# ScalarE copies of the up half, Sigmoid for tanh, and new engine orders in a transformer block with linear attention and a gated MLP

## Chip, core and metric

The kernel runs on one core of a Trainium2 chip. The metric is the device time of one execution in microseconds (us). Of several executions the median counts. The five engines each work through their own queue in order: TensorE (PE in the profile, with its weight loads as PEld), VectorE (DVE), ScalarE (ACT), GpSimd (POOL) and SyncE (SP), which here issues nearly all DMAs.

## What is computed

The input x is 2048 rows of 448 (bfloat16). A linear attention with 16 heads of 28 and then a gated MLP are added to it, each behind a layernorm:

```python
q, k, v = split_heads(layernorm(x) @ wqkv)
pq, pk  = q @ w_phi, k @ w_phi                      # per head, 28 x 28
phi_q   = concat(softmax(pq), softmax(-pq))         # phi_k in the same way
kv, z   = sum_s phi_k[s]^T v[s], sum_s phi_k[s]
h       = x + concat_heads((phi_q @ kv) / (phi_q @ z + 1e-6)) @ wo
n       = layernorm(h)
out     = h + (sigmoid(n @ w_gate) * (n @ w_up)) @ w_down   # 448 -> 1792 -> 448
```

## The kernel before

The 2048 rows are 16 tiles (t = 0 to 15) of 128. The kernel is written as a list of named operations, each with what it reads and writes; from that list the waits on semaphores are derived (a DMA has a semaphore of its own in a ring; whoever needs several loads waits for each). The order of the operations on each engine isn't derived: it is written out by hand in ORDER, one string per engine. An engine does its operations strictly in that order, so one that waits holds up all behind it.

The names that matter below, with the engine and the line of the profile:

- x0 to x14, ld_k, ld_v, ld_q0 to ld_q3 on SP load the input and A_wqkv. The four ld_q are transposing DMAs (L503) into WqT.
- bst, agg, pow1, nm1, nb1, xn (L548 to L579) are the first layernorm on VectorE, GpSimd and ScalarE; xn5 and its like write xn_pad, which has five buffers. xT0 to xT3 transpose it on TensorE (with a copy xT0e to xT3e on ScalarE or VectorE), xT4 to xT15 do so by DMA (L586).
- w2m0_0 to w2m0_3 and w2m1_0 to w2m1_3 (TensorE, L615) fold w_phi into wk and wq. Each w2m1 reads all four parts of WqT. w2e are the copies out of PSUM.
- ppa, ppb, pva, pvb, vva, vvb (TensorE, helper line L329) are the products with Wk and wv: 8 matmuls of 448 columns in the a part, 6 in the b part. The array is used as two halves of 64 rows that write two PSUM banks at the same time; the b part swaps the banks of the halves, so it waits until the a part is done with them. v1_t copies v out of PSUM (L534), ek_t takes exp (L674, L675), ss, rs, phi (L678 to L688) normalise it, kva_t and kvb_t add phi^T v into banks 6 and 7, which seed starts.
- warm0 to warm9 are matmuls on zeros that fill TensorE's time at the start.
- pqa, pqb (TensorE) and eq (ScalarE, L726, exp of 1024 columns) make phi_q; num_t (TensorE) the numerators and sums in banks 6 and 7 (num1 in 2 and 3); rsm, qq, b, c, rden (VectorE, L803 to L811) and o_t (GpSimd or VectorE, L815) the quotient; oT_t its transpose (by DMA from t = 2 on, L828); wof0, wof1, woa, wob (TensorE) the product with wo in banks 2 and 3.
- h_t (VectorE, L841) adds x and gives the row sum; h0 and h1 are copies on ScalarE. nm, sq (ScalarE Square, L847), ve (L850), pow2 (GpSimd, L852), hn (L856) are the second layernorm, hT_t the transpose (by DMA, L864).
- wwo and wgu are operations on TensorE without an instruction: they only wait, for the four loads of wo and for the eight loads of the gate and up weights.
- ga and gb (TensorE, L329) are gate and up of one group: ga0_5 is tiles 0 and 1 (256 columns), column block ff = 5 of 14; the groups of tiles 0 and 2 have 256 columns, those of tiles 4, 8 and 12 have 512. An even ff has its gate in bank 4 and its up half in bank 5, an odd one in banks 0 and 1, so a group can start when the one before the last has been read out. sig (ScalarE, L914) and hh (VectorE, L915) read them out: sig writes sg_sb, which has four buffers, and hh reads sg_sb and the up bank and writes hhT.
- dn, dp, dm, dl (TensorE) are the down product, fin (VectorE, L949) adds it to h, out_t stores.

The operations are made in the order of PROGRAM; ORDER interleaves them, for instance the gate groups of tiles 0 and 1 with num and wo of later tiles. Before, the sigmoid is made as (tanh(g/2) + 1) / 2: hh is (tanh + 1) times up, and fin multiplies by 0.5:

```python
op("act", "sig" + nm, lambda e: e.activation(sg_sb[:, k, 0:N], bk(bg)[:, 0:N], ACT.Tanh, scale=0.5), r=[B(bg)], w=[("sg", k)])
op("dve", "hh" + nm, lambda e: e.scalar_tensor_tensor(out=hhT[(t0 // 4) % NHH][:, ff, ns], in0=sg_sb[:, k, 0:N], scalar=1.0,
                                                      in1=bk(bu)[:, 0:N], op0=ALU.add, op1=ALU.mult), ...)
```

tanh and exp need no change of ScalarE's function tables between them: the trace has one table load, at the start.

Of the kernel before, what the change touches and what calls it, by code (L numbers as in the profile page):

```python
# [1020 lines left out]
```

## Time and profile before

| | us |
|---|---|
| median of 3 runs (lowest, highest) | 203.37 (203.37, 203.64) |
| the profiled execution's own time | 203.38 |
| span from its first to its last instruction | 201.6 |
| TensorE busy in the span | 195.6 |

The granted clock of TensorE is 1.00 throughout. "Busy" counts instructions that are under way; matmuls overlap and their ends are modelled, so busy time says where TensorE stood still, not how fast it was. A row of the table by stages gives the stretch, its length, and then the busy time and count for PE, PEld, DVE, ACT and POOL, the clock, the DMA share and GB/s. A row of a timeline gives start, duration, engine, line, operation, out<-in, and in brackets the idle time ahead of it and what ended it. A row of the waits gives who waited for whom, the total, the times and the longest. A row of the groups gives line, engine, operation, operands and shape, the count, then busy us, mean ns of one, and the idle time before. Names of operations aren't in the trace: they are read off by counting a queue's instructions along ORDER.

### The profile page before, as it was taken

To read this page: it belongs to the slowest core of one execution; us is meant where nothing else is said; L and a number is where in the kernel's file an instruction comes from. 1 tells how busy PE (TensorE), PEld (TensorE's weight loads), DVE (VectorE), ACT (ScalarE), POOL (GpSimd) and SP (SyncE) were. 2 spreads that over 40 slices of the span, in tenths; PEclk is the share of its full clock that TensorE was granted. 3 is DMA by queue.
4 is the path that set the end of the run, shared out by engine and by line. 5 is a ranking of instruction groups with operands and counts; after the bars stand their busy time and mean duration, and the time that the engine had idled before them with its cause. 6 is when DMAs were issued, how large, how long until landed. Compare 5 with 4: busy or idle time off the path is not lost.

```text
span 201.6 us, 5849 instructions
## 1 busy us (share of the span) xinstructions
PE 195.6 (97%) x2500; PEld 114.0 (57%) x2500; DVE 133.1 (66%) x326; ACT 91.7 (45%) x189; POOL 57.4 (28%) x90
## 2 busy tenths in 40 slices
PE   7989999999979999999999999999999999999995
PEld 2935565665558788776444444555555555444443
DVE  6998999978999984496758877436432422272224
ACT  3778988998672663222333442324322212222220
POOL 5689869913531962000041110001400000000000
DMA  6967554919994246130005411030222000004002
GB/s 169 301 136 134 58 80 86 295 55 270 313 204 92 52 57 80 27 41 17 0 3 114 87 31 25 7 71 23 60 49 52 0 0 3 0 3 137 0 0 91
DMA packets 32866, 16.25 MB, mean 81 GB/s; under 512 B 25096, under 2 KB 31944, under 8 KB 32840
## 3 DMA queue, kind: packets, MB, share of 16 engines
q1 hardware_dynamic: 32336, 15.86, 34.9%
q8 instruction: 19, 0.31, 0.7%
q10 hardware_dynamic: 504, 0.03, 0.2%
q14 instruction: 7, 0.06, 0.1%
HBM read 8.34 MB, written 1.84 MB: 50 GB/s over the span
## 4 chain that ended last, share of the span: by engine, by line
PE 89%; SPq 5%; DMA 2%; ACT 2%; issue 1%; DVE 0%
PE psum L329 82%; PE psum L942 5%; SPq L430 3%; DMA WqT<-in_A_wqkv_dram 2%; SPq L503 2%; ACT eq L726 2%; PE psum L890 1%; PE psum L541 0%; DVE v L534 0%; PE psum L615 0%; PE psum L888 0%; DVE x_sb L949 0%
## 5 line engine op out<-in xcount | busy, mean ns | idle before, releaser
L329 PE MATMUL psum<-xnT,wg_sb 64*128 64x512 bf16 (+1 forms) x490 | 93.1, 333 | 0.4 <-ACT eq L726 0.2
L329 PE MATMUL psum<-xnT,wu_sb 64*128 64x512 bf16 (+1 forms) x490 | 92.8, 333 | 0.0
L914 ACT ACTIVATE sg_sb<-psum 128x512 bf16<-128x512 f32 (+1 forms) x70 | 34.9, 511 | 90.5 <-PE psum L329 90.0
L915 DVE SCALAR_TENSOR_TENSOR hhT<-sg_sb,psum 128x512 bf16<-128x512 bf16 (+1 forms) x70 | 39.0, 577 | 53.8 <-ACT sg_sb L914 53.1
L329 PEld LDWEIGHTS psum<-xnT,wg_sb 64*128 64x128 bf16 x490 | 44.5, 94 | 21.5 <-DVE hhT L915 3.1
L329 PEld LDWEIGHTS psum<-xnT,wu_sb 64*128 64x128 bf16 x490 | 44.5, 94 | 12.8
L329 PE MATMUL psum<-wd_sb,hhT 64*128 64x448 bf16 x336 | 36.9, 349 | 0.0
L329 PEld LDWEIGHTS psum<-wd_sb,hhT 64*128 64x128 bf16 x336 | 17.8, 94 | 14.3 <-DVE x_sb L841 0.5
L329 PE MATMUL psum<-wv_sb,xnT 64*128 64x448 bf16 x112 | 22.3, 351 | 0.1
L329 PE MATMUL psum<-Wk,xnT 64*128 64x448 bf16 x112 | 22.1, 350 | 0.2 <-DVE v L534 0.2
L850 POOL TENSOR_SCALAR ve<-ssq 128x1 f32<-128x1 f32 x10 | 2.0, 201 | 61.2 <-ACT junk L847 60.9
L688 POOL TENSOR_TENSOR phi<-hhT,rs 128x896 bf16<-128x896 bf16 x10 | 17.1, 1724 | 2.2 <-PE psum L329 1.4
L678 DVE TENSOR_REDUCE ss<-hhT 128x32 f32<-128x896 bf16 x16 | 16.9, 1067 | 0.3 <-ACT hhT L675 0.3
L726 ACT ACTIVATE eq<-psum 120x1024 bf16<-120x1024 f32 x16 | 15.7, 1032 | 1.0 <-PE psum L329 0.9
L329 PE MATMUL psum<-xnT,Wq 64*120 64x512 bf16 x112 | 14.8, 384 | 0.2
L815 POOL TENSOR_TENSOR o_pad<-c_sb,rden 128x448 bf16<-128x448 bf16 x12 | 11.1, 934 | 13.5 <-DVE rden L811 13.4
L329 PE MATMUL psum<-wo_e,oT 64*128 64x448 bf16 x49 | 11.5, 349 | 0.0
L329 PE MATMUL psum<-wo_o,oT 64*128 64x448 bf16 x49 | 11.5, 349 | 0.0
L942 PE MATMUL psum<-wd_sb,hhT 128*128 128x448 bf16 (+2 forms) x70 | 11.1, 316 | 0.0
L949 DVE SCALAR_TENSOR_TENSOR x_sb<-psum,x_sb 128x448 bf16<-128x448 f32 (+2 forms) x17 | 9.4, 591 | 2.5 <-PE psum L942 1.6
L806 DVE TENSOR_TENSOR b_sb<-psum,qq 128x464 bf16<-128x464 f32 x16 | 10.1, 637 | 0.7 <-PE psum L329 0.4
L329 PEld LDWEIGHTS psum<-Wk,xnT 64*128 64x128 bf16 x112 | 7.6, 94 | 4.9 <-issue 1.4
(107 smaller groups left out, 230.8 us busy)
## 6 DMA issues: line engine op xcount, KB each, us to landing
out_dram<-x_sb SPq DMA_DIRECT2D x15, 112.0 KB, 1.8
...
```

The costliest lines, as they stand in the source:

```text
L329: p = e.matmul(o, lhsT=w, rhs=r, start=st, stop=sp, tile_position=(row, 0))
L430: return op(eng, name, lambda e: e.dma_start(dst, src), r=r, w=w, dma="in" if eng == "sp" else "ain", nring=48 if eng == "sp" else 8, kb=kb)
L503: op("sp", "ld_q%d" % gg, lambda e, gg=gg: e.dma_start_transpose(out=WT[1][:, gg:gg + 1, :], in_=A_wqkv[:, gg * GP:gg * GP + P]), w=[("WqT ...
L678: op("dve", "ss%d" % t, lambda e: e.tensor_reduce(ss[:, s, :].rearrange("p (b h) -> p b h", h=2), eks.rearrange("p b (d h) -> p b h d", h= ...
L688: return e.tensor_tensor(phi[:, sp, :, :, :].rearrange("p b a n -> p (b a) n")[:, :, 0:56].rearrange("p b (d h) -> p b d h", h=2), eks.rea ...
L726: op("act", "eq%d_%d%s" % (c, i, "pm"[sg]), lambda e, sg=sg: e.activation(eq[c][:, sg, 2 * i:2 * i + 2, :].rearrange("p g n -> p (g n)"), ...
L806: op("dve", "b%d" % t, lambda e: e.tensor_tensor(h3(b_sb), OMv[:, :, :, 0:EV], h2(qq)[:, :, :, None].to_broadcast([P, NB, 8, EV]), ALU.mul ...
L815: return e.tensor_tensor(o_pad[:, t % NO, off:off + D].rearrange("p (h d) -> p h d", h=H), c_sb[:, t % NS, :, 0:DH], rden[:, t % NS, :][:, ...
L914: op("act", "sig" + nm, lambda e: e.activation(sg_sb[:, k, 0:N], bk(bg)[:, 0:N], ACT.Tanh, scale=0.5), r=[B(bg)], w=[("sg", k)])
L915: op("dve", "hh" + nm, lambda e: e.scalar_tensor_tensor(out=hhT[(t0 // 4) % NHH][:, ff, ns], in0=sg_sb[:, k, 0:N], scalar=1.0, in1=bk(bu)[ ...
L942: p = e.matmul(bk(b)[:, lo:hi], lhsT=hb[:, ff, TS(t)], rhs=wd_sb[:, ff, lo:hi], start=ff == 0, stop=ff == FT - 1)
L949: op("dve", "fin%d%s" % (t, nm), lambda e: e.scalar_tensor_tensor(out=h_sb[:, t, lo:hi], in0=bk(b)[:, lo:hi], scalar=0.5, in1=h_sb[:, t, l ...
```

## The change

Sigmoid takes the place of tanh, so hh becomes one product and fin multiplies by 1.0. For 26 of the 28 groups of 256 columns (UCOPY: all but 0_0 and 0_1), ScalarE copies the up half out of PSUM to SBUF (uc, into xn_pad, which is free by then), and hh reads two SBUF operands, on VectorE or, for 12 of them, on GpSimd, which ORDER decides. sload is one sigmoid of one column that stands behind the last eq. The four loads of wo share one semaphore, and so do the eight of gate and up. The orders of all engines are new up to about the groups of tile 4; behind that they are the same.

```diff
+        if many is not None:
+            o.sem, o.val = (dma,) + many[:1], 16 * many[1]
...
+        op("act", "sload", lambda e: e.activation(sg_sb[:, 0, 0:1], neghalf[:, 0:1], ACT.Sigmoid), r=["neghalf"], w=[("sg", 0)])
...
-            op("act", "sig" + nm, lambda e: e.activation(sg_sb[:, k, 0:N], bk(bg)[:, 0:N], ACT.Tanh, scale=0.5), r=[B(bg)], w=[("sg", k)])
-            op("dve", "hh" + nm, lambda e: e.scalar_tensor_tensor(out=hhT[(t0 // 4) % NHH][:, ff, ns], in0=sg_sb[:, k, 0:N], scalar=1.0,
-                                                                  in1=bk(bu)[:, 0:N], op0=ALU.add, op1=ALU.mult),
-               r=[B(bu), ("sg", k)], w=[("hh", (t0 // 4) % NHH, ff, t % 4) for t in range(t0, t0 + n)])
+            op("act", "sig" + nm, lambda e: e.activation(sg_sb[:, k, 0:N], bk(bg)[:, 0:N], ACT.Sigmoid), r=[B(bg)], w=[("sg", k)])
+            up, ub = bk(bu)[:, 0:N], B(bu)
+            if nm in UCOPY:
+                j = UCOPY.index(nm) % NX
+                up, ub = xn_pad[:, j, 0:N], ("xn", j)
+                op("act", "uc" + nm, lambda e: e.copy(up, bk(bu)[:, 0:N]), r=[B(bu)], w=[ub])
+            op(("pool", "dve") if nm in UCOPY else "dve", "hh" + nm, lambda e: e.tensor_tensor(
+                hhT[(t0 // 4) % NHH][:, ff, ns], sg_sb[:, k, 0:N], up, ALU.mult),
+               r=[ub, ("sg", k)], w=[("hh", (t0 // 4) % NHH, ff, t % 4) for t in range(t0, t0 + n)])
```

The orders, cut to what is spoken of below:

```diff
 pe (before)
-w2m0_3 warm6 warm7 warm8 ppa0 xT3 ppb0 xT2 warm9 vva0 seed vvb0 ppa2 w2m1_0 w2m1_1 vva2 ppb2 vvb2 kva0 w2m1_3 w2m1_2 pva4 pvb4 kvb1 pva5
-pqb1_1 num0 num1 ... oT1 wwo wof0 wof1 ... hT0 hT1 num6 wgu ga0_1 ga0_0
-ga2_4 ga2_5 gb2_4 gb2_5 dp0_8 dp0_11 ga2_6 ga2_7
 pe (after)
+w2m0_3 warm6 warm7 warm8 warm9 ppa0 xT2 ppb0 vva0 xT3 vvb0 w2m1_1 w2m1_0 ppa2 vva2 ppb2 vvb2 w2m1_2 seed w2m1_3 pva4 kvb0 pvb4 kva1 pva5
+pqb1_1 wwo num0 num1 ... oT1 wof0 wof1 ... hT0 hT1 wgu num6 ga0_1 ga0_0
+ga2_4 dp0_4 ga2_5 gb2_4 dp0_8 gb2_5 dp0_11 ga2_6 ga2_7
 act (before)
-w2e0_0 w2e0_2 w2e0_3 xT3e nm1_4 ek0 ek1 ... ek2 nm1_8 ek3 v1_3
-eq3_0p eq3_0m eq3_1p eq3_1m sig0_1 sig0_0 sig0_3 sig0_2
-sq4 sq5 sig0_11 sig0_10 sq7 sig0_13 sq6 sig0_12 sig2_1
 act (after)
+w2e0_0 w2e0_2 nm1_2 w2e0_3 nm1_3 xT2e ek0 ek1 ... ek2 ek3 v1_3 nm1_8
+eq3_0m eq3_0p eq3_1p eq3_1m sload sig0_1 sig0_0 sig0_3 uc0_3 uc0_2 sig0_2
+sq4 sq5 sig0_13 uc0_12 sig0_12 uc0_13 sq6 sq7 uc2_0 ... uc2_4 sig2_5 uc2_5 uc2_6 sig2_6
 pool (before)
-o0 o1 o2 o3 pow2_0 pow2_1 o4 o5 nm2 o6 o7 pow2_3 ve2 pow2_2 hn3 hn2 ve5 o8 nm4 pow2_4 o9 nm5 pow2_5 pow2_7 pow2_6 ve8
 pool (after)
+o0 o1 o2 o3 pow2_1 pow2_0 o5 o4 o7 ve2 hh0_2 pow2_2 hh0_4 hh0_5 o8 hh0_7 hn2 ve3 pow2_3 hn3 nm6
+o9 ve6 ve4 hh0_12 pow2_6 ve5 hn6 hh2_0 pow2_4 hn4 ve7 pow2_7 pow2_5 hn5 hh2_3 hh2_1 hh2_6 hh2_7 hh2_8 hh2_9 ve8
 dve (after, the hh of UCOPY among them)
+rden7 hh0_3 h2 h3 rden6 o6 rsm8 ... h5 qq9 hh0_6 ... h7 hh0_9 h6 hh0_8 rsm10 rden9 hh0_13 hh0_10 qq10 nm5 hh0_11 nm7 hh2_2
```

SP's order changes only from oT4 on (oT5 oT4 oT7 oT6 oT8 hT2 hT3 ... in place of oT4 oT5 oT6 oT7 hT3 hT2 ...).

More of the change, by code (lines that the diff above doesn't have):

```diff
@@ L28, in __init__, with op @@
         self.where = {n: e for e in ENGINES for n in ORDER[e].split()}
-    def op(self, eng, name, fn, r=(), w=(), dma=None, nring=0, after=(), rows=128, half=None, kb=0, grp=None):
+    def op(self, eng, name, fn, r=(), w=(), dma=None, nring=0, after=(), rows=128, half=None, kb=0, grp=None, many=None):
         o = _Op()
@@ L309 @@
 PACE = {"ld_wg1": "kva14"}
+UCOPY = "0_2 0_3 0_4 0_5 0_6 0_7 0_8 0_9 0_10 0_11 0_12 0_13 2_0 2_1 2_2 2_3 2_4 2_5 2_6 2_7 2_8 2_9 2_10 2_11 2_12 2_13".split()
 PROGRAM = (
@@ L427, in B, with load @@
             return ("bank", i)
-        def load(name, dst, src, w, kb, r=(), eng="sp"):
+        def load(name, dst, src, w, kb, r=(), eng="sp", many=None):
             return op(eng, name, lambda e: e.dma_start(dst, src), r=r, w=w, dma="in" if eng == "sp" else "ain",
-                      nring=48 if eng == "sp" else 8, kb=kb)
+                      nring=(48 if eng == "sp" else 8) if many is None else 0, kb=kb, many=many)
         op("dve", "zero", lambda e: e.memset(zero[:], 0.0), w=["zero"])
@@ L504, in build @@
                 out=WT[1][:, gg:gg + 1, :], in_=A_wqkv[:, gg * GP:gg * GP + P]), w=[("WqT", gg)], dma="tr", nring=64)
-        load("ld_woe0", wo_e[:, 0:3, :], A_wo[0:3 * P, :].rearrange("(kt p) n -> p kt n", p=P), [("wo", 0)], 336)
-        load("ld_woe1", wo_e[0:64, 3, :], A_wo[3 * P:D, :], [("wo", 1)], 56)
-        load("ld_woo0", wo_o[:, 1:4, :], A_wo[64:D, :].rearrange("(kt p) n -> p kt n", p=P), [("wo", 2)], 336)
-        load("ld_woo1", wo_o[64:P, 0, :], A_wo[0:64, :], [("wo", 3)], 56)
+        load("ld_woe0", wo_e[:, 0:3, :], A_wo[0:3 * P, :].rearrange("(kt p) n -> p kt n", p=P), [("wo", 0)], 336, many=(100, 4))
+        load("ld_woe1", wo_e[0:64, 3, :], A_wo[3 * P:D, :], [("wo", 1)], 56, many=(100, 4))
+        load("ld_woo0", wo_o[:, 1:4, :], A_wo[64:D, :].rearrange("(kt p) n -> p kt n", p=P), [("wo", 2)], 336, many=(100, 4))
+        load("ld_woo1", wo_o[64:P, 0, :], A_wo[0:64, :], [("wo", 3)], 56, many=(100, 4))
         wo_keys = [("wo", i) for i in range(4)]
@@ L518, in build @@
                 load("ld_%s%d" % (nm, kt), dst[part, kt, :], src[r0 + part.start:r0 + part.stop, :], [(nm, kt)],
-                     448 * (part.stop - part.start) // P)
+                     448 * (part.stop - part.start) // P, many=(101, 2 * KT))
                 wgu_keys.append((nm, kt))
@@ L949, in finish @@
             op("dve", "fin%d%s" % (t, nm), lambda e: e.scalar_tensor_tensor(
-                out=h_sb[:, t, lo:hi], in0=bk(b)[:, lo:hi], scalar=0.5, in1=h_sb[:, t, lo:hi], op0=ALU.mult, op1=ALU.add),
+                out=h_sb[:, t, lo:hi], in0=bk(b)[:, lo:hi], scalar=1.0, in1=h_sb[:, t, lo:hi], op0=ALU.mult, op1=ALU.add),
                r=[B(b), ("x", t)], w=[("xo", t, lo)])
```

79 rows, old and new, of the table ORDER are left out of this document.

## The prediction

> **What bounds the kernel now.** I read the engine totals first, then the table by stages, then the waits, then the chain of work that ended last.
>
> ```profile
> PE 195.6 (97%) x2500; PEld 114.0 (57%) x2500; DVE 133.1 (66%) x326; ACT 91.7 (45%) x189; POOL 57.4 (28%) x90
> ```
> ```profile
> 20.00:44.00 24.00, 23.94 (x449) 14.75 (x443) 22.50 (x44) 22.10 (x45) 18.59 (x13) 1.00 0.54 119
> ...
> 59.20:76.70 17.50, 17.43 (x320) 14.03 (x322) 15.66 (x52) 8.80 (x26) 10.81 (x19) 1.00 0.38 72
> 76.70:95.00 18.30, 18.30 (x292) 14.31 (x290) 11.67 (x35) 4.92 (x14) 0.31 (x1) 1.00 0.31 42
> ```
> ```profile
> PE psum L615 <- DMA WqT<-in_A_wqkv_dram: 0.7, 1, 0.7
> ```
> ```profile
> 10.72 4.12 DMA WqT<-in_A_wqkv_dram
> ...
> 19.30 24.18 PE psum L329 x431
> ```
>
> The reader is to see three things. TensorE has 0.06 us of idle time between 20 and 44, 0.07 between 59.2 and 76.7 and none between 76.7 and 95: in the two gate stages that the 26 groups belong to (59 to 95), where VectorE is busy 15.66 of 17.5 and 11.67 of 18.3 us, nothing of that reaches TensorE. So relief for VectorE has almost nothing to win there. What TensorE loses, it loses before 20 us, where the chain runs through the last load of WqT, and at a few joints. So the question of this change is what its **new orders** do at those joints.
>
> **The start.** Here are TensorE's instructions around the wait for WqT, and VectorE's one that ends the next wait.
>
> ```profile
> 13.33 0.93 PE L329 MATMUL psum<-Wk,xnT 64*128 64x448 bf16 x8
> 14.98 0.55 PE L615 MATMUL psum<-Wphi,WqT 112*128 112x112 bf16 x8 [0.72 <-DMA WqT<-in_A_wqkv_dram]
> 15.46 0.93 PE L329 MATMUL psum<-wv_sb,xnT 64*128 64x448 bf16 x8
> 16.23 0.73 PE L329 MATMUL psum<-Wk,xnT 64*128 64x448 bf16 x6
> 16.80 0.73 PE L329 MATMUL psum<-wv_sb,xnT 64*128 64x448 bf16 x6
> 17.36 0.28 PE L329 MATMUL psum<-v,phi 64*128 64x58 bf16 x8
> 17.57 0.57 PE L615 MATMUL psum<-Wphi,WqT 112*128 112x112 bf16 x8
> 18.30 0.35 PE L329 MATMUL psum<-Wk,xnT 64*128 64x448 bf16 x1 [0.16 <-DVE v L534]
> ```
> ```profile
> 17.57 0.63 DVE L534 CAST v<-psum 128x448 bf16<-128x448 f32 x1 [0.85 <-PE psum L329]
> ```
>
> By the order of before these are ppa2, w2m1_0 with w2m1_1, vva2, ppb2, vvb2, kva0, w2m1_3 with w2m1_2, pva4. Slots, start to start: vva2 0.77, ppb2 0.57, vvb2 0.56, the pair w2m1_0/1 0.48; ppa2 has as many matmuls of the same width as vva2, so 0.77. The WqT loads keep their place in SP's queue, and w2m1 needs all four, so it can't begin before about 14.98 in either kernel. Before, ppa2 is done under that wait. After, **w2m1_1 and w2m1_0 stand ahead of ppa2**, and seed moves behind the wait too. TensorE then arrives at 13.33 at the latest, where ppa2 starts now, and some 0.2 earlier with seed's two matmuls gone from there: it idles 1.65 to 1.9 us. From 14.98, 0.48 for w2m1 and 0.77 + 0.77 + 0.57 + 0.56 for ppa2, vva2, ppb2, vvb2 bring vvb2's slot to its end at 18.13. v1_2 on VectorE, which frees the bank that pva4 writes, follows 0.2 behind that slot's end (17.57 against 17.36) and pva4 0.73 behind v1_2's start (18.30 against 17.57): pva4 at 19.07, 0.77 later than now. seed and the other w2m1 fit into that step, as kva0 and they do now. A little comes back: pva4 and pvb4 had stood side by side, with a stop for the other half's bank (pvb4 at 19.30, 1.00 after 18.30, against 0.77: 0.23); after, kvb0 stands between them. kva0's 0.21 is still to do and takes the most of it again. I take **+0.7**. Bounds: +0.3 if ppa2's delay is half absorbed behind v1_2, +1.1 if seed and ppa2 come on top whole. Nothing later gives it back, since 20 to 44 has 0.06 us idle. The exchange of two xT and nm1 instructions between ScalarE, GpSimd and VectorE in this stage fills time in which TensorE idles: 0. nm1_8 goes behind v1_3 on ScalarE, and xn8, xn9, phi2 and xn11 on GpSimd and four transposes in SP's queue go later with it; I cost that at 0 too, because TensorE's own shift by 0.7 covers about half and these tiles are made ahead of use; uncovered, pva8 would wait, by an estimate up to 0.5, which the upper bound takes in.
>
> **The gate's first groups.** The wait for eight loads (wgu) becomes one semaphore and moves ahead of num6, under a wait for VectorE's c_sb; wwo likewise moves to where TensorE has a backlog. In exchange ScalarE switches tables once (sload) between the last eq and sig0_1.
>
> ```profile
> 55.41 3.77 ACT L726 ACTIVATE eq<-psum 120x1024 bf16<-120x1024 f32 x4 [0.24 <-PE psum L329]
> 60.64 0.71 ACT L914 ACTIVATE sg_sb<-psum 128x256 bf16<-128x256 f32 x2 [1.46 <-PE psum L329]
> ```
> ```profile
> 61.05 0.75 DVE L915 SCALAR_TENSOR_TENSOR hhT<-sg_sb,psum 128x256 bf16<-128x256 bf16 x2 [0.23 <-ACT sg_sb L914]
> ```
> ```profile
> L476 ACT ACT_TABLE_LOAD x1 | 1.3, 1283 | 3.4 <-DVE mask L468 3.4
> ```
> ```profile
> PEld psum L329 <- DVE c_sb L809: 1.0, 1, 1.0
> ...
> PE psum L329 <- ACT eq L726: 0.2, 1, 0.2
> ```
>
> The last fence is the wait view of 57 to 59.5: num6 waits 1.0 for c_sb, and then TensorE idles 0.2 more between num6 and ga0_1, which I put down to wgu's waits: up to 0.25 to win. ScalarE ends eq at 59.18, has 1.46 us free and starts sig0_1 at 60.64. After: 1.28 for the load and about 0.25 for sload's own one column give 60.7 to 60.8, so sig0_1 starts 0.1 later than now instead of 0.25 earlier, hh0_1 behind it too, and with it the bank that the next odd group needs. The gain of 0.25 and the table cancel: I take **0**, between -0.25 (table wholly covered) and +0.2. The Trainium skill, ScalarE: Activation LUTs, section What ACT_TABLE_LOAD costs, says that a switch is 1283 ns and a drain of about 1380 ns, 2.66 us; the trace agrees on the first (1283) and has no row for the second. By 2.66 this term would be about +1.3 rather than 0.
>
> The joint at 70.5 goes. There the first instruction of woa6 waits for oT7:
>
> ```profile
> 67.96 1.26 SPq L828 DMA_TRANSPOSE oT<-o_pad  x1
> ```
> ```profile
> 70.23 0.27 PE L329 MATMUL psum<-xnT,wg_sb 64*128 64x256 bf16 x1
> 70.54 0.35 PE L329 MATMUL psum<-wo_e,oT 64*128 64x448 bf16 x1
> ```
> ```profile
> oT<-o_pad SPq DMA_TRANSPOSE x14, 2.5
> ```
>
> Issued at 67.96, 2.5 us to land: 70.46, and woa6 at 70.54, when the last gate matmul (70.23 and 0.27) had drained, where undisturbed ones overlap: about 0.2 of the 0.31 between the two starts is lost. After, GpSimd makes o7 right after o4 and VectorE makes o6, so both transposes are issued some 1.5 us sooner: **-0.2**.
>
> **Copies and products.** 26 copies like the sigmoids of 128x256 (0.33 to 0.36 each, since 0.71 covers two) add 8.6 us to ScalarE, whose 59.2 to 95 has 13.7 of 35.8 busy: covered, and banks come free in time (four ScalarE instructions per pair of groups, 1.4 us, against 2.5 of TensorE for each of the seven pairs of the first stage). 26 hh of 417 ns leave VectorE; 14 come back. Their cost isn't in the trace: at least 0.18 (by the row of phi below, 637 x 256/896), at most 0.42; 0.25 taken, as phi too reads SBUF alone. It is on no path. 12 go to GpSimd:
>
> ```profile
> L688 POOL TENSOR_TENSOR phi<-hhT,rs 128x896 bf16<-128x896 bf16 x10 | 17.1, 1724 | 2.2 <-PE psum L329 1.4 <-DVE rs L684 0.7
> ...
> L815 POOL TENSOR_TENSOR o_pad<-c_sb,rden 128x448 bf16<-128x448 bf16 x12 | 11.1, 934 | 13.5 <-DVE rden L811 13.4
> L915 DVE SCALAR_TENSOR_TENSOR hhT<-sg_sb,psum 128x256 bf16<-128x256 bf16 x28 | 10.8, 417 | 7.0 <-ACT sg_sb L914 6.6
> ...
> L847 ACT ACTIVATE junk<-x_sb,sum 128x448 bf16<-128x448 bf16 x14 | 9.2, 659 | 1.1 <-DVE x_sb L841 1.0
> ...
> L852 POOL TENSOR_TENSOR rst<-ve,neghalf 128x1 f32<-128x1 f32 x14 | 7.6, 551 | 0.5
> ...
> L688 DVE TENSOR_TENSOR phi<-hhT,rs 128x896 bf16<-128x896 bf16 x6 | 3.7, 637 | 0.1
> ...
> L850 POOL TENSOR_SCALAR ve<-ssq 128x1 f32<-128x1 f32 x10 | 2.0, 201 | 61.2 <-ACT junk L847 60.9
> ...
> L856 POOL TENSOR_SCALAR hn_pad<-x_sb,nm,rst 128x512 bf16<-128x512 bf16 x2 | 1.5, 770 | 0.0
> ```
>
> 896 columns 1724 ns, 448 columns 934: 1.76 ns a column and 0.14 fixed, so 0.60 us for 256. **GpSimd becomes a queue that reaches TensorE**: sg_sb has four buffers, so sig2_5 must wait for hh2_1, and ga2_7 for sig2_5 and uc2_5. hh2_1 stands behind ve6, ve4, hh0_12, pow2_6, ve5, hn6, hh2_0, pow2_4, hn4, ve7, pow2_7, pow2_5, hn5, hh2_3, and ve6 behind sq6.
>
> ```profile
> 75.06 0.27 PE L329 MATMUL psum<-xnT,wg_sb 64*128 64x256 bf16 x1
> ...
> 85.47 0.27 PE L329 MATMUL psum<-xnT,wg_sb 64*128 64x256 bf16 x1
> ```
> ```profile
> 83.79 0.71 ACT L914 ACTIVATE sg_sb<-psum 128x256 bf16<-128x256 f32 x2 [2.06 <-PE psum L329]
> ```
>
> The first row ends gb0_12 at 75.33, the second starts ga2_7. After gb0_12 ScalarE has uc0_12, sig0_12, uc0_13 (1.1) and sq6 (0.66): 77.1. GpSimd's list: 4 ve (0.8), 4 pow2 (2.2), 3 hn (2.3), 4 hh (2.4) make 7.7: hh2_1 ends near 84.8 to 84.9. sig2_5, which would start near 84.7 (0.57 later than the 84.1 that the row of 83.79 gives, as dp0_8, six matmuls like ppb2's, is put ahead of gb2_5), goes to 84.95 with uc2_5, uc2_6 and sig2_6 queued behind it, uc2_5 ends near 85.7, ga2_7 at 85.77: **+0.3**, between 0 and +0.9 (next part). tanh and Sigmoid, and hh on PSUM as one product, I cost alike (0); factor 0.5 in fin too.
>
> **Sum** against the profiled execution's own 203.38 (span 201.6 and 1.8 around it; the median of the runs is 203.37): 0.7 + 0 - 0.2 + 0.3 = +0.8. **Forecast 204.2 us**, likeliest range 203.8 to 204.8.
>
> **Rivals.** *The wait for WqT isn't longer* (the other side). WqT's last load was issued at 10.72 and took 4.12. If such a transpose landed in the 2.8 us that the ones of xnT take,
>
> ```profile
> xnT<-xn_pad SPq DMA_TRANSPOSE x12, 2.8
> ```
>
> it would be there at 13.5, 1.3 earlier, and the order that starts w2m1 first would gain: 0.7 - 1.3 + 0.1 gives **202.9**. It decides from a landing before 14.0 on, 0.8 earlier than now. For it: the wide spread of such loads; against: SP's queue in front of it is unchanged. *Half paid*: the start costs 0.3 and the table hides, so the joints outweigh: 0.3 - 0.25 - 0.2 + 0.1, **203.3**. *GpSimd's queue is slower than its rows*: in before, a GpSimd phi that ran beside a VectorE phi shows a pair of 3.71 where two means make 3.45, and a pair of xn 1.88 against 1.54 for two of hn's 770, which has the same size.
>
> ```profile
> 34.06 3.71 POOL L688 TENSOR_TENSOR phi<-hhT,rs 128x896 bf16<-128x896 bf16 x2
> 18.54 1.88 POOL L579 TENSOR_SCALAR xn_pad<-x_sb,nm,rst 128x512 bf16<-128x512 bf16 x2
> ```
>
> At 0.3 for each of two or three VectorE products that fall into that queue, ga2_7 is 0.6 to 0.8 later yet: **204.9**. The Trainium skill, SBUF — State Buffer, section Who interferes with whom, says it as a rule: a VectorE instruction with two SBUF inputs and a GpSimd instruction that reads SBUF exclude each other. The two rows agree. *The switch is longer*: if ScalarE stands still around the load for as long again as it lasts (1.28), sig0_1, hh0_1 and ga0_3 are 1.3 later: 204.2 + 1.3, **205.5**; for it, no row shows a load with work in flight; against, the one load there cost 1283 ns. *It doesn't do what it says*: were Square not in Sigmoid's table, 14 squares at two loads of 1.28 add 36 us to ScalarE, and the time is over 210.
>
> **Chances.** Forecast 0.49, GpSimd's queue 0.10, longer switch 0.06, tables flipping 0.02, WqT early 0.18, half paid 0.15. About 0.2%, 0.41 us, is what a measurement of this kernel can tell from no change. Slower (above 203.78): nearly all of the forecast with the three behind it, 0.66; within 0.2%: 0.16; faster: 0.18. The range from 202.9 to 205.3 leaves out the two long-table cases and half of the early one.
>
> **What would show it.** The wait of L615 for WqT in the after trace: 1.7 to 2.0 us (0.72 now), and pva4 near 19.1; if that wait is under 1.0, the forecast falls. ACT_TABLE_LOAD twice, the second at 59.9 to 61.5 (all marks after 20 us lie 0.8 later than now). No idle time ahead of woa6. A wait of sig2_5 for GpSimd's hh, and TensorE idle 0.2 to 0.5 us ahead of ga2_7. The stage after 95 us keeps its length.

## The result and the profile after

The changed kernel takes **204.74 us** (median of 22 runs, 204.12 to 205.90), the kernel before 203.69 us on the same chip (22 runs, 203.05 to 205.91): a ratio of 1.005, 95% interval 1.0032 to 1.0069. It is 1.05 us slower; 0.8 was forecast. The kernel before stands 0.3 higher in this series than in the 3 runs that the forecast of 204.2 started from, so it is the differences that are compared. A second series on another occasion (the run e5_changed_again below) gives 204.42 against 203.39, +1.03.

The profiled execution of the first series took 205.90 us, the slowest of its 22 runs. The totals of its page:

```profile
PE 195.4 (96%) x2500; PEld 112.7 (55%) x2500; DVE 127.1 (62%) x310; ACT 99.8 (49%) x217; POOL 67.1 (33%) x106
```

VectorE has 6.0 us less to do, ScalarE 8.1 and GpSimd 9.7 more, and TensorE as much as before. To see what TensorE makes of that, cut both traces at the same instructions of TensorE: pva4, num0, then hT1, dn0_0, ga4_1 and the end. These are the tables by stages of before, then of the changed kernel (its second profile, of 204.08 us). The columns are those of the prediction's table; the second number is the length of the stretch.

```profile
18.30:45.73 27.43, 27.30 (x505) 16.64 (x507) 25.82 (x50) 25.30 (x53) 20.23 (x15) 1.00 0.55 117
57.32:75.15 17.83, 16.66 (x325) 13.57 (x324) 16.49 (x53) 9.41 (x26) 9.37 (x15) 1.00 0.47 98
75.15:94.85 19.70, 19.70 (x308) 15.17 (x306) 12.57 (x39) 6.18 (x19) 1.86 (x5) 1.00 0.30 42
94.85:201.60 106.75, 104.29 (x1024) 52.57 (x1020) 52.28 (x111) 30.26 (x58) 7.74 (x18) 1.00 0.15 36
```

```profile
18.74:46.17 27.43, 27.37 (x514) 16.94 (x514) 26.13 (x50) 25.34 (x54) 21.09 (x16) 1.00 0.58 117
57.70:75.01 17.31, 16.35 (x327) 13.75 (x325) 14.56 (x48) 12.51 (x36) 9.63 (x15) 1.00 0.45 105
75.01:95.56 20.55, 19.81 (x309) 13.96 (x306) 7.99 (x29) 11.17 (x38) 11.41 (x21) 1.00 0.17 35
95.56:202.30 106.74, 104.28 (x1024) 52.58 (x1022) 52.61 (x112) 30.27 (x58) 7.75 (x18) 1.00 0.15 36
```

The reader is to see that the attention stage and everything behind ga4_1 keep their length to 0.01 us. The first gate stage is 0.52 us shorter, the second 0.85 us **longer**, although VectorE is busy 4.6 us less in it: TensorE was never idle there before and now is for 0.7. Between num0 and hT1, which the tables leave out, 57.70 less 46.17 is 11.53, where before had 57.32 less 45.73, 11.59: -0.06. From pva4 to the end that makes -0.06 - 0.52 + 0.85 - 0.01, **+0.26**. The remaining 0.8 of the 1.05 lie ahead of pva4.

There the first profile shows the wait that the prediction is about, and the instructions behind it (w2m1_1 and w2m1_0, ppa2, vva2, ..., vvb2, and pva4):

```profile
15.19 0.55 PE L619 MATMUL psum<-Wphi,WqT 112*128 112x112 bf16 x8 [1.43 <-DMA WqT<-in_A_wqkv_dram]
15.68 0.93 PE L333 MATMUL psum<-Wk,xnT 64*128 64x448 bf16 x8
...
17.77 0.73 PE L333 MATMUL psum<-wv_sb,xnT 64*128 64x448 bf16 x6
18.43 0.37 PE L619 MATMUL psum<-Wphi,WqT 112*128 112x112 bf16 x4
...
19.34 0.36 PE L333 MATMUL psum<-Wk,xnT 64*128 64x448 bf16 x1
```

The wait is 1.43 us (0.72 before), ppa2 begins at 15.68 instead of 13.33, and pva4 at 19.34 instead of 18.30. The second profile, whose last WqT arrived earlier, has the same picture with less wait:

```profile
14.59 0.55 PE L619 MATMUL psum<-Wphi,WqT 112*128 112x112 bf16 x8 [0.66 <-DMA WqT<-in_A_wqkv_dram]
```

In the second gate stage, these are GpSimd's queue from ve6 and ve4 to hh2_3 and hh2_1, ScalarE's sig2_5 and uc2_5, and TensorE's last matmul of ga2_6 and first of ga2_7, all in the first profile:

```profile
78.66 0.46 POOL L854 TENSOR_SCALAR ve<-ssq 128x1 f32<-128x1 f32 x2 [0.61 <-ACT junk L851]
79.18 0.67 POOL L925 TENSOR_TENSOR hhT<-sg_sb,xn_pad 128x256 bf16<-128x256 bf16 x1
79.80 0.57 POOL L856 TENSOR_TENSOR rst<-ve,neghalf 128x1 f32<-128x1 f32 x1
80.45 0.19 POOL L854 TENSOR_SCALAR ve<-ssq 128x1 f32<-128x1 f32 x1
80.73 0.77 POOL L860 TENSOR_SCALAR hn_pad<-x_sb,nm,rst 128x512 bf16<-128x512 bf16 x1
...
85.10 0.77 POOL L860 TENSOR_SCALAR hn_pad<-x_sb,nm,rst 128x512 bf16<-128x512 bf16 x1 [0.18 <-POOL rst L856]
85.83 1.29 POOL L925 TENSOR_TENSOR hhT<-sg_sb,xn_pad 128x256 bf16<-128x256 bf16 x2
```
```profile
87.22 0.38 ACT L919 ACTIVATE sg_sb<-psum 128x256 bf16<-128x256 f32 x1 [1.16 <-PE psum L333]
87.50 0.37 ACT L924 CAST xn_pad<-psum 128x256 bf16<-128x256 f32 x1
```
```profile
86.94 0.27 PE L333 MATMUL psum<-xnT,wu_sb 64*128 64x256 bf16 x1
87.92 0.28 PE L333 MATMUL psum<-xnT,wg_sb 64*128 64x256 bf16 x1 [0.72 <-ACT xn_pad L924]
```

Read it backwards: ga2_7 at 87.92 waits for uc2_5 (87.50 and 0.37), which stands behind sig2_5 on ScalarE; sig2_5 starts at 87.22, 0.1 after GpSimd's hh2_1 has ended (85.83 and 1.29: 87.12). The bracket of sig2_5 names TensorE, whose gate half had been done for a microsecond (the last matmul of gb2_5 ends at 86.20); what came last is GpSimd. From ga2_6 to ga2_7 TensorE takes 1.31 us; before, it took 0.44.

One thing in the first profile belongs to no step: a stop of TensorE in the middle of kvb13, with no semaphore to wait for.

```profile
43.99 0.21 PE L333 MATMUL psum<-v,phi 64*128 64x58 bf16 x3
45.06 1.01 PE L333 MATMUL psum<-v,phi 64*128 64x58 bf16 x37 [0.86 <-issue]
```

It is 0.86 us long, and pva4 to num0 takes 28.55 us there instead of 27.43. The profiled execution is 2.5 us above the profiled one of before; the medians, 1.05 apart, are what is explained here.

### The profile page after: what moved, and what is told of

It is laid out like the page before. It is cut to its first block, busy times and chain, and to the rows that moved or that the text cites. A ratio compares the mean times of both kernels' runs of the same rounds, so it can differ in the third digit from the quotient of the medians.

```text
span 204.0 us, 5889 instructions
## 1 busy us (share of the span) xinstructions
PE 195.4 (96%) x2500; PEld 112.7 (55%) x2500; DVE 127.1 (62%) x310; ACT 99.8 (49%) x217; POOL 67.1 (33%) x106
## 4 chain that ended last, share of the span: by engine, by line
PE 89%; SPq 5%; DMA 2%; issue 1%; DVE 1%; ACT 0%
PE psum L333 82%; PE psum L952 5%; SPq L434 3%; DMA WqT<-in_A_wqkv_dram 2%; SPq L507 2%; PE psum L894 1%; PE psum L619 1%; PE psum L545 0%; DVE b_sb L810 0%; DVE c_sb L813 0%; PE psum L892 0%; ACT sg_sb L919 0%; DVE xnT L538 0%; PE psum L716 0%; DVE x_sb L959 0%
## 5 line engine op out<-in xcount | busy, mean ns | idle before, releaser
L919 ACT ACTIVATE sg_sb<-psum 128x512 bf16<-128x512 f32 (+1 forms) x70 | 35.7, 516 | 80.4 <-PE psum L333 79.9
L925 DVE TENSOR_TENSOR hhT<-sg_sb,psum 128x512 bf16<-128x512 bf16 (+1 forms) x44 | 28.9, 671 | 46.8 <-ACT sg_sb L919 46.5
L854 POOL TENSOR_SCALAR ve<-ssq 128x1 f32<-128x1 f32 x14 | 3.1, 222 | 47.0 <-ACT junk L851 46.4
L819 POOL TENSOR_TENSOR o_pad<-c_sb,rden 128x448 bf16<-128x448 bf16 x11 | 10.2, 935 | 17.2 <-DVE rden L815 17.1
L845 DVE SCALAR_TENSOR_TENSOR x_sb<-psum,x_sb 128x448 bf16<-128x448 f32 x14 | 8.3, 620 | 5.9 <-PE psum L333 5.8
L924 ACT CAST xn_pad<-psum 128x256 bf16<-128x256 f32 x26 | 9.5, 379 | 3.0 <-PE psum L333 3.0
```

The lines of the kernel that those rows point to most:

```text
L819: return e.tensor_tensor(o_pad[:, t % NO, off:off + D].rearrange("p (h d) -> p h d", h=H), c_sb[:, t % NS, :, 0:DH], rden[:, t % NS, :][:, ...
L845: op("dve", "h%d" % t, lambda e: e.scalar_tensor_tensor(out=h_sb[:, t, :], in0=bk(b)[:, 0:D], scalar=1.0, in1=x_sb[:, t, :], op0=ALU.mult, ...
L924: op("act", "uc" + nm, lambda e: e.copy(up, bk(bu)[:, 0:N]), r=[B(bu)], w=[ub])
L925: op(("pool", "dve") if nm in UCOPY else "dve", "hh" + nm, lambda e: e.tensor_tensor(hhT[(t0 // 4) % NHH][:, ff, ns], sg_sb[:, k, 0:N], up ...
```

## The experiments

**Theory.** TensorE is one chain, and the change puts two losses on it, at the start (WqT with ppa2 behind it) and ahead of ga2_7 (GpSimd's queue), and takes two away (wgu, woa6); losses in series add. **Rivals:** the loss is spread over the program or is that stop of kvb13; one joint hides the other; the table switch or the semaphores act otherwise than costed. Each kernel was timed beside the kernel before on the same chip; the difference of the medians and the 95% interval of the ratio are given. A difference has an uncertainty of about 0.4 us, so the traces, cut into stages as above, decide where a gain sits.

| run | us | before | difference | ratio, 95% | trace, pva4 to the end against before |
|---|---|---|---|---|---|
| changed (first series) | 204.74 | 203.69 | +1.05 | 1.0032 to 1.0069 | +0.25 (without the stop's 1.12) |
| e5_changed_again | 204.42 | 203.39 | +1.03 | 1.0011 to 1.0056 | +0.26 |
| e1_ppa2_first | 204.07 | 203.24 | +0.83 | 1.0018 to 1.0055 | +0.26 |
| e2_hh21_dve | 203.85 | 203.24 | +0.61 | 1.0008 to 1.0046 | -0.61 |
| e11_hh21_early | 203.92 | 203.41 | +0.51 | 1.0012 to 1.0052 | -0.65 |
| e3_both | 203.13 | 203.24 | -0.11 | 0.9976 to 1.0015 | -0.66 |
| e10_seed | 203.24 | 203.41 | -0.17 | 0.9972 to 1.0015 | -0.65 |
| e12_pe_start | 204.05 | 203.49 | +0.56 | 1.0015 to 1.0047 | -0.55 |
| e6_before_start | 203.06 | 203.39 | -0.33 | 0.9961 to 1.0003 | -0.40 |
| e4_before_w2m1 | 204.08 | 203.24 | +0.84 | 1.0022 to 1.0061 | -0.03 |
| e7_before_sem | 202.91 | 203.39 | -0.48 | 0.9942 to 0.9996 | -0.31 |
| e8_before_sigmoid | 203.44 | 203.39 | +0.05 | 0.9982 to 1.0020 | -0.07 |
| e9_sem_o7 | 203.10 | 203.41 | -0.31 | 0.9969 to 0.9999 | +0.10 |

The last column is worked out from the starts of pva4 and the end of the last matmul: before has 18.30 to 199.24, 180.94 us. What the median has beyond it (+0.8 for the changed kernel) happened ahead of pva4.

**The changed kernel again.**

> The changed kernel itself once more, beside the three others and on the same chip as they. Theory (two joints in series: 0.7 at the start and 0.9 ahead of ga2_7, less 0.3 at num6 and 0.2 at woa6): +1.1 to +1.5 us against the kernel before. The stop of 0.86 us in the middle of kvb13 that the first profile of it showed doesn't come back if it was an event of that one execution; if it belongs to the program, it stands at the same place again.

+1.03, a little under what was expected, and kvb13 runs through without a stop. So the stop was an event of one execution, and it is no part of the 1.05; the rival that puts the loss there falls.

**The start, by one move.** ppa2 goes back ahead of w2m1:

```diff
-ppa0 xT2 ppb0 vva0 xT3 vvb0 w2m1_1 w2m1_0 ppa2 vva2
+ppa0 xT2 ppb0 vva0 xT3 vvb0 ppa2 w2m1_1 w2m1_0 vva2
```

> The changed kernel with ppa2 put back ahead of w2m1_1 and w2m1_0 in TensorE's order, nothing else. Theory (the loss sits at two joints: the start, where TensorE waits for WqT with ppa2 still undone, and the joint before ga2_7): TensorE's wait for WqT falls from 1.4 us to about 0.7, and the time falls by 0.7 us against the changed kernel (0.5 to 0.8), to about 204.0. Rival (the loss is spread, by stops of TensorE that no semaphore explains or by a slower clock of the whole program): 0 to -0.2. Rival (the start's loss is swallowed by a later wait, on v1 or xnT): wait shorter, pva6 earlier by less than 0.3, time -0.2 or less.

Only 0.2 is won (1.03 and 1.05 become 0.83), where 0.5 to 0.8 was expected. The wait for WqT is gone from the profile; in its place TensorE waits ahead of ppa2 for ScalarE's exponential:

```profile
14.19 0.93 PE L333 MATMUL psum<-Wk,xnT 64*128 64x448 bf16 x8 [0.28 <-ACT hhT L679]
15.18 0.55 PE L619 MATMUL psum<-Wphi,WqT 112*128 112x112 bf16 x8
```

So the theory was too simple at the start: there is a second wait behind the first one. The reverse edit in the kernel before:

```diff
-vvb0 ppa2 w2m1_0 w2m1_1 vva2
+vvb0 w2m1_0 w2m1_1 ppa2 vva2
```

> The kernel before with one edit: w2m1_0 and w2m1_1 put ahead of ppa2 in TensorE's order. Theory: the wait for WqT grows from 0.7 to 1.4 to 1.6 us, and the time by 0.6 to 0.8 us against the kernel before (about 204.4). Rival (the order alone doesn't matter; the start of the changed kernel is late because its first loads or transposes come later): 0 to +0.2.

+0.84, the whole 0.8 by this one exchange. Its profile alone would have misled: there WqT came early.

```profile
14.11 0.55 PE L615 MATMUL psum<-Wphi,WqT 112*128 112x112 bf16 x8 [0.32 <-DMA WqT<-in_A_wqkv_dram]
```

w2m1 could begin at 14.11 here, at 14.59 and 15.19 in the two profiles of the changed kernel, at 14.98 in that of before. The landing of this load differs by a microsecond between executions, the profiled one is the fastest of e4's twelve runs (203.24), and only the median tells what an order costs that exposes TensorE to it. What the order does behind the landing, each trace does show. From w2m1's start to pva4's TensorE takes 3.32 us in before (14.98 to 18.30) and 3.39 in e1 (15.18 to 18.57), with ppa2 already done; it takes 4.08 in e4 (14.11 to 18.19) and 4.15 in both profiles of the changed kernel and in those of e2 and e11 (14.75 to 18.90), with ppa2 still to do. That is 0.76 to 0.83 more, whenever WqT lands.

**GpSimd's queue.** hh2_1 moves to VectorE; or stays on GpSimd, but stands earlier.

```diff
 pool (e2)
-pow2_5 hn5 hh2_3 hh2_1 hh2_6
+pow2_5 hn5 hh2_3 hh2_6
 dve (e2)
-hh0_11 nm7 hh2_2
+hh0_11 nm7 hh2_1 hh2_2
 pool (e11, in place of both)
-hn6 hh2_0 pow2_4 hn4 ve7 pow2_7 pow2_5 hn5 hh2_3 hh2_1 hh2_6
+hn6 hh2_0 hh2_1 pow2_4 hn4 ve7 pow2_7 pow2_5 hn5 hh2_3 hh2_6
```

> The changed kernel with hh2_1 alone moved from GpSimd's queue to VectorE's (ahead of hh2_2), so that sig2_5 no longer waits for the end of GpSimd's queue. Theory: the 0.88 us that TensorE loses between ga2_6 and ga2_7 shrinks to 0 to 0.2, time -0.6 to -0.9 us against the changed kernel, to about 204.0. Rival (hh2_1 is not what the chain hangs on; the next joint in the queue, hh2_3 and sig2_7, takes its place, since hh2_3 still ends at about the same time): half of it, -0.3 to -0.4, with a new idle stretch ahead of ga2_8 or ga2_9. Rival (spread loss): 0.

> The changed kernel with hh2_1 kept on GpSimd but put right behind hh2_0 in its queue, ahead of pow2_4, hn4, ve7, pow2_7, pow2_5, hn5 and hh2_3. Theory (it is the place in the queue, not GpSimd's speed, that makes ga2_7 late): TensorE's 0.9 ahead of ga2_7 goes as it did with hh2_1 on VectorE, +0.2 to +0.6 against the kernel before, where the changed kernel stands at +1.03; hn4, hn5 and hh2_3 end 0.7 later and nobody waits for them. Rival (GpSimd is too slow for these products anywhere): the stall of 0.9 stays, or moves to ga2_8 or ga2_9 or to the transposes of hn ahead of ga4_1: +0.8 or more.

Both take the stop away. In e11, where GpSimd still makes all twelve products, TensorE goes from ga2_6 into ga2_7 (85.48) without a wait, and hh2_1, now in the second place of a pair, ends at 81.2:

```profile
85.37 0.27 PE L333 MATMUL psum<-xnT,wu_sb 64*128 64x256 bf16 x1
85.48 0.27 PE L333 MATMUL psum<-xnT,wg_sb 64*128 64x256 bf16 x1
```
```profile
79.92 1.30 POOL L925 TENSOR_TENSOR hhT<-sg_sb,xn_pad 128x256 bf16<-128x256 bf16 x2
```

The trace from pva4 on falls by 0.87 (e2) and 0.92 (e11) against the changed kernel's, and no new stop appears at ga2_8, ga2_9 or ga4_1. So it was the **place in the queue**. The medians fell by 0.4 and 0.5, less than the traces say; within the uncertainty of 0.4 they agree.

**Both edits.**

> Both edits: ppa2 ahead of w2m1_1, and hh2_1 on VectorE. Theory (two joints in series on TensorE's one path): the gains add, -1.3 to -1.6 us against the changed kernel, 203.2 to 203.4, which is 0.3 to 0.5 below the kernel before. Rival (one joint covers the other, so that what is won at the start is lost again by waiting for ScalarE or GpSimd later): no more than the better of the two alone, -0.7, and 204.0, still above the kernel before.

-0.11 against before, 1.14 to 1.16 below the changed kernel: more than either edit alone, so the rival of one joint hiding the other falls. It is even 0.5 more than the two edits win one by one (0.2 and 0.4); no trace explains that, and it is about the uncertainty. But against before 0.2 to 0.4 of what was expected is missing, and the trace says where: from pva4 on this kernel is 0.66 faster than before, so 0.55 is still lost ahead of pva4.

**What is left at the start.** All five engines get the order of before up to the end of the attention sums (e6); only seed is put back (e10); only TensorE's order is put back (e12).

```diff
 pe (e10, from e3)
-xT3 vvb0 ppa2 w2m1_1 w2m1_0 vva2 ppb2 vvb2 w2m1_2 seed w2m1_3 pva4
+xT3 seed vvb0 ppa2 w2m1_1 w2m1_0 vva2 ppb2 vvb2 w2m1_2 w2m1_3 pva4
 pe (e12, from e3)
-warm9 ppa0 xT2 ppb0 vva0 xT3 vvb0 ppa2 ... vvb2 w2m1_2 seed w2m1_3 pva4 kvb0 ...
+ppa0 xT3 ppb0 xT2 warm9 vva0 seed vvb0 ppa2 ... vvb2 kva0 w2m1_3 w2m1_2 pva4 pvb4 ...
```

> The kernel with both edits (ppa2 first, hh2_1 on VectorE), and on all five engines the order of the kernel before up to the end of the attention sums (as far as pqb1_1 on TensorE, eq3_1m on ScalarE, kvz on VectorE, phi13 on GpSimd); from there on the orders of the changed kernel. Theory: the new order of the start holds a second loss that the wait for WqT had hidden, ScalarE's k exponential standing behind nm1_2 and nm1_3, which makes TensorE wait 0.3 us ahead of ppa2; with the old start that is gone too, and 0.3 at num6 and 0.2 at woa6 are won: -0.4 to -0.7 against the kernel before. Rival (the start's orders are equal once ppa2 is back in its place): the same time as with both edits, 0 to -0.2 against the kernel before.

> The kernel with both edits (ppa2 first, hh2_1 on VectorE; -0.11 us against the kernel before), and seed moved back from between w2m1_2 and w2m1_3 to ahead of vvb0. Theory (with seed gone from there TensorE comes to ppa2 early, waits 0.3 for ScalarE's exponential, and does seed later, where it costs its 0.2 to 0.3): the wait of 0.28 ahead of ppa2 nearly goes, warm8 to pva4 falls from 9.0 to about 8.75 us, and the time to -0.3 to -0.4 against the kernel before. Rival (what is left of the start's loss is the other engines' new orders): no change by seed, 0 to -0.1 against the kernel before.

> The kernel with both edits (-0.11 us against the kernel before), with TensorE's order of the kernel before up to pqb1_1, and ScalarE, VectorE, GpSimd and SP in the order of the change. (With all five engines' old order it was -0.33.) Theory: what is left of the start's loss, 0.3 us from warm8 to pva4 (9.0 against 8.7 where WqT isn't waited for), lies in TensorE's own order: warm9 ahead of ppa0, and seed and w2m1 ahead of pva4 one by one: warm8 to pva4 at 8.7 plus the wait for WqT, and -0.3 to -0.5 against the kernel before. Rival (it lies in the other engines' order, which makes xn2 and xn3, or the exponentials, later than TensorE's old order wants them): TensorE waits at xT3 or ppa2, warm8 to pva4 9.0 or more without a wait for WqT, 0 to -0.1 or slower.

With the whole old start (e6) the time falls by a further 0.2. That alone is within the uncertainty, and the -0.33 is short of the -0.4 to -0.7 expected. But e6's trace loses 0.26 behind pva4 that e3's doesn't (0.2 of it between dn0_0 and ga2_0, 1.71 against 1.51), and what the median (-0.33) has beyond the trace (-0.40) is 0.07: as far as that split can tell, the start's loss is gone. Neither partial move does that. seed in e10 stands right behind xT3 and waits for VectorE's copy of xT3's result out of PSUM; warm8 to pva4 takes 9.49 us, not the 8.75 expected:

```profile
13.39 0.27 PE L716 MATMUL psum<-epsr,epsl 64*128 64x232 bf16 x1 [0.79 <-DVE xnT L538]
```

and TensorE's old order among the new orders of the others (e12) is slower, +0.56, as that run's rival had it: it asks for xT3 first, GpSimd makes xn2 first, and ScalarE's exponentials follow late.

```profile
11.38 0.40 PE L545 MATMUL psum<-ident,xn_pad 128*128 128x128 bf16 x4 [0.29 <-POOL xn_pad L583]
...
15.22 0.93 PE L333 MATMUL psum<-Wk,xnT 64*128 64x448 bf16 x8 [0.37 <-ACT hhT L679]
```

So the orders of the engines fit together as a set, and what is left is not TensorE's order alone, as the theory of that run had it. Which of the other engines' moves costs the rest isn't settled. The traces put 0.3 of it between warm8 and pva4 (9.51 to 18.57 in e1 and 11.57 to 20.53 in e3, about 9.0, where e7 and e8, which also have no wait for WqT, take 8.68, and e6 8.74 without its wait of 0.26); the difference to the 0.55 is within the uncertainty of a median. warm8 itself begins between 8.85 and 9.69, in e3 at 11.57, behind the first loads; whether the change has a part in that, single traces can't tell.

**The semaphores and the table, each alone on the kernel before.**

```diff
 (e7: many= for the loads of wo and of gate and up, as in the change)
-num3 oT1 wwo wof0 ... hT1 num6 wgu ga0_1
+wwo num0 ... num3 oT1 wof0 ... hT1 wgu num6 ga0_1
```
```diff
 (e8; the factor in fin becomes 1.0 too)
-ACT.Tanh, scale=0.5
+ACT.Sigmoid
-scalar_tensor_tensor(..., scalar=1.0, in1=bk(bu)[:, 0:N], op0=ALU.add, op1=ALU.mult)
+tensor_tensor(..., sg_sb[:, k, 0:N], bk(bu)[:, 0:N], ALU.mult)
-... eq3_1p eq3_1m sig0_1
+... eq3_1p eq3_1m sload sig0_1
```

> The kernel before with one semaphore each for the four wo loads and the eight gate and up loads, and wwo and wgu at their new places in TensorE's order; tanh and everything else as before. Theory: num6's slot falls from 0.65 to 0.33 us, time -0.25 to -0.35 against the kernel before. Rival (TensorE's 0.3 between num6 and ga0_1 isn't wgu's waits but ga0_1's wait for a bank, from ScalarE's eq): slot unchanged, 0.

> The kernel before with Sigmoid for tanh alone: sload's table switch between eq3_1m and sig0_1, hh as one product of sg_sb and the up half in PSUM, factor 1.0 in fin; no copies of the up half, no product on GpSimd. Theory: ScalarE has 1.46 us free there, the switch takes 1.28 and its one column 0.2, sig0_1 starts at most 0.1 later: 0 to +0.2 against the kernel before. Rival (a switch also waits for the work in flight to drain, as long again): sig0_1 1.3 later, +1.0 to +1.3.

e7 is -0.48, the fastest of all, and its interval lies wholly below 1: **a version that beats both kernels**, with a handful of lines of the change. (e9, which holds the same lines, has -0.31 and an interval below 1 too.) The trace gives 0.31 of it from pva4 on: in it hT1 to dn0_0 is 0.22 shorter and num0 to hT1 0.07. num6 now runs into ga0_1, and ScalarE's last four eq stand beside it:

```profile
58.30 0.40 PE L331 MATMUL psum<-kvz,eq 56*128 56x60 bf16 x16 [0.96 <-DVE c_sb L811]
58.64 0.27 PE L331 MATMUL psum<-xnT,wg_sb 64*128 64x256 bf16 x1
```
```profile
55.05 3.77 ACT L728 ACTIVATE eq<-psum 120x1024 bf16<-120x1024 f32 x4 [0.24 <-PE psum L331]
```

0.34 from one to the other, where before took 0.65 (58.58 to 59.23). A little of that is paid ahead of num6, where the one wait of wgu stands now (1.34 from hT1 to num6, 1.26 before). The bracket in before named ScalarE's eq for the 0.25, since the last eq ended at 59.18, just ahead of ga0_1 (59.23). But here ga0_1 starts at 58.64, 0.18 before the last eq ends (55.05 and 3.77: 58.82). So it doesn't wait for that eq, and the rival falls: with the eight waits gone from that place the 0.25 is gone too.

e8 changes nothing (+0.05). Its ScalarE around the switch:

```profile
58.54 1.28 ACT L898 ACT_TABLE_LOAD   x1
59.84 0.21 ACT L898 ACTIVATE sg_sb<-neghalf 128x1 bf16<-128x1 f32 x1
59.94 0.76 ACT L915 ACTIVATE sg_sb<-psum 128x256 bf16<-128x256 f32 x2
```

The load starts 0.02 after the last eq has ended (54.75 and 3.77: 58.52), lasts 1.28, and is followed at once; sig0_1 stands 3.28 behind TensorE's hT1 (56.66), before it stood 3.32 behind (57.32 and 60.64). And the product as one operation on a PSUM operand takes 418 ns, as the two operations did (417).

**The joint at woa6 alone**, on top of e7:

```diff
 dve
-c7 hh0_3 hh0_2 h2 h3 rden6 rden7 rsm8
+c7 rden7 hh0_3 hh0_2 h2 h3 rden6 rsm8
 pool, sp
-o4 o5 nm2 o6 o7 pow2_3   /   oT4 oT5 oT6 oT7
+o4 o5 o7 nm2 o6 pow2_3   /   oT4 oT5 oT7 oT6
```

> The kernel before with the semaphores and the places of wwo and wgu of the change (as in the run before, -0.48 us there), and o7 and rden7 made ahead of o6 and rden6, its transpose ahead of oT6's, so that woa6 no longer waits; tanh, start and products as before. Theory: the joint at woa6 is worth 0.2 and adds to the semaphores' 0.3: -0.5 to -0.7 against the kernel before, lower than every kernel so far. Rival (the joint only moves to the next transposed tile or bank): -0.3 to -0.5, as the semaphores alone, with a new idle stretch ahead of woa6, wob6 or dn0_0.

The time is the rival's, and so is the mechanism, that the joint only moves; but it moves to a place that the rival didn't name. woa6 starts 0.18 behind the last gate matmul (0.32 in e7, 0.09 in the changed kernel), but rden7 ahead of hh0_3 on VectorE makes hh0_3 late, and ga0_5 with it:

```profile
63.47 0.41 PE L331 MATMUL psum<-kvz,eq 56*128 56x60 bf16 x16
64.02 0.28 PE L331 MATMUL psum<-xnT,wg_sb 64*128 64x256 bf16 x1
```

```profile
PEld psum L331 <- DVE hhT L917: 0.3, 1, 0.3
```

num8 takes 0.55 to ga0_5 instead of the 0.32 of before and e7 (0.23 in the changed kernel), and ga0_5 to dn0_0 gets only 0.13 shorter. (The other 0.3 of the last column's +0.10 is a wait of 0.2 for VectorE's phi behind pvb4, ahead of everything that the edit touches.) The changed kernel has rden7 in the same place and doesn't pay that; there uc0_3 on ScalarE, not hh0_3, frees the bank. That this is the reason is argued from the order and wasn't tried; if it is, it is the one place where a copy is worth something to TensorE.

## Why the prediction was right, and where it wasn't

**The sum** was +0.8, measured +1.05. The direction and most of the size came from naming the joints of TensorE. By its own steps:

**The start, +0.7: right in size.** The median has 0.8 ahead of pva4, e4 gives 0.84 by the exchange of w2m1 and ppa2 alone, and pva4 stands at 19.34 and 18.74 about the 19.07 worked out. The mechanism holds: ppa2 isn't done under the wait any more, and w2m1 to pva4 takes 4.15 us, where the working had 4.09 (14.98 to 19.07). Two parts of the step didn't hold. The wait was put at 1.65 to 1.9 us, with TensorE there at 13.33 or earlier and WqT at 14.98. It was 1.43 (13.76 to 15.19) and 0.66 (13.93 to 14.59): TensorE came later, with ppa0 at 10.07 and 10.24 instead of 9.44, and the landing moves by a microsecond. The sign "if that wait is under 1.0, the forecast falls" was a bad one: the second profile has 0.66, and its run +1.03. And the sentence that "the exchange of two xT and nm1 instructions between ScalarE, GpSimd and VectorE in this stage fills time in which TensorE idles: 0" failed: with the wait for WqT taken away, 0.5 of the 0.8 stays (e1, e3, e10), and of the moves tried only the whole old start brings it back (e6, as far as medians tell). The two losses overlap: e4 has the one without the other, e1 the other without the one, and together they make less than their sum. In e2 and e11, which start as the changed kernel does, the median has 1.2 ahead of pva4 and not 0.8; the split is no finer than that.

**The gate's first groups, 0: wrong, it is -0.3.** The step that failed is "the gain of 0.25 and the table cancel". The gain came (e7), and the table cost nothing (e8). The working took it that a sig0_1 that comes 0.35 us too late for an earlier ga0_1 makes the next odd group late. In the first profile ScalarE does this,

```profile
57.50 3.77 ACT L730 ACTIVATE eq<-psum 120x1024 bf16<-120x1024 f32 x4
61.29 1.28 ACT L902 ACT_TABLE_LOAD   x1
62.58 0.20 ACT L902 ACTIVATE sg_sb<-neghalf 128x1 bf16<-128x1 f32 x1
62.69 0.64 ACT L919 ACTIVATE sg_sb<-psum 128x256 bf16<-128x256 f32 x2
```

and sig0_1 does come 1.6 behind ga0_1 (61.09) instead of 1.41, but ga0_3 follows ga0_1 by 2.52, as before by 2.51: with gb0_1, gb0_0, woa2 and num7 in between, the bank had time to spare. The estimate of sload, 0.25, was 0.20. So the waits and the switch had the sizes that were worked out; that the switch would eat up the gain is what failed. The rival of the longer switch falls with it: the Trainium skill, ScalarE: Activation LUTs, section What ACT_TABLE_LOAD costs, adds a drain of about 1380 ns to the 1283; the rows of this kernel and of e8 show 1.28, 0.01 to 0.02 between the load and its neighbours, and no drain; 1.3 more would stand in the medians, and e8 has +0.05.

**The joint at 70.5, -0.2: right.** woa6 (72.08 in the first profile) follows the last gate matmul by 0.09, where before had 0.31:

```profile
71.99 0.27 PE L333 MATMUL psum<-xnT,wg_sb 64*128 64x256 bf16 x1
72.08 0.35 PE L333 MATMUL psum<-wo_e,oT 64*128 64x448 bf16 x1
```

Of the 0.52 that the first gate stage wins, 0.23 is num6, 0.21 this joint and 0.08 ga0_5. That the move isn't free by itself, e9 shows.

**GpSimd's queue, +0.3: the chain was right, its length too short.** The measured loss is 0.85, just inside the bounds 0 to 0.9. TensorE idles 0.72 ahead of ga2_7, where 0.2 to 0.5 was named. Beginning: 77.1 was forecast in marks of before, where dn0_0 stands at 75.15; in the first profile it stands at 76.72, 1.57 later, and ve6 at 78.66, as forecast (78.67). But the queue from there to the end of hh2_1 takes 8.46 us (87.12 less 78.66) and not 7.7. The twelve rows of that stretch, five of which are left out above, sum to 7.96, since the products are 0.67 each instead of 0.60 (a straight line through 448 and 896 columns was too low); the other 0.50 are gaps of 0.05 to 0.2 us between one GpSimd instruction and the next, as the 0.18 in the row at 85.10 shows, which a sum of durations leaves out. So sig2_5 came 0.70 later than forecast (87.22 against 84.95 and 1.57) and ga2_7 0.58 (87.92 against 85.77 and 1.57): that is the missing part of the term.

```profile
L924 ACT CAST xn_pad<-psum 128x256 bf16<-128x256 f32 x26 | 9.5, 379 | 3.0 <-PE psum L333 3.0
...
L925 POOL TENSOR_TENSOR hhT<-sg_sb,xn_pad 128x256 bf16<-128x256 bf16 x12 | 7.8, 667 | 3.7 <-ACT sg_sb L919 2.5 <-ACT xn_pad L924 1.0
...
L925 DVE TENSOR_TENSOR hhT<-sg_sb,xn_pad 128x256 bf16<-128x256 bf16 x14 | 4.1, 306 | 6.9 <-ACT xn_pad L924 6.9
```

These are the groups of the copies and of the two kinds of products. The rival that GpSimd runs slower than its rows beside VectorE has its mechanism in this trace, but not in this queue. VectorE's hh2_2 and GpSimd's hn4 meet in the first profile:

```profile
82.99 0.67 DVE L925 TENSOR_TENSOR hhT<-sg_sb,xn_pad 128x256 bf16<-128x256 bf16 x1 [4.15 <-ACT xn_pad L924]
```
```profile
82.75 0.77 POOL L860 TENSOR_SCALAR hn_pad<-x_sb,nm,rst 128x512 bf16<-128x512 bf16 x1
```

Here VectorE pays: 0.67, where its 13 other products take 0.23 to 0.30. GpSimd's hn4, which began first, keeps its 0.77. At 67.48 it is the other way round: GpSimd's ve2, begun 0.14 after VectorE's o6, takes 0.53 instead of 0.19. In the queue from ve6 to hh2_1 no GpSimd instruction is lengthened so: hn and pow2 have the durations of before, and the products take 0.67 whether VectorE is busy beside them or not. So the rival's price wasn't paid, and e11 with the same work on GpSimd loses nothing at ga2_7. That ga2_7 came 0.58 later than forecast, near the rival's 0.6 to 0.8, has another cause, the gaps and the low estimate.

**Copies and products, 0: right.** 26 copies of 379 ns and the products at 306 ns on VectorE (0.25 was taken, 0.18 to 0.42 allowed) leave VectorE 4.6 us less busy in the second gate stage, and TensorE gets next to nothing for it: e3 with all of it and e7 without differ by 0.35 from pva4 on, and 0.30 of that is woa6 and ga0_5.

**Together:** 0.8 ahead of pva4, -0.06 by wwo, -0.52 and +0.85 in the gate stages. The forecast had the gate's gain too small by 0.3 and GpSimd's loss too small by 0.55; the two errors half cancel in the sum, so that it comes within 0.25 is in part luck.
